# Order of weight conversion, sums of squares and normalisations in the first two blocks of a linear attention, cosine FFN and soft MoE kernel

## Chip, cores and metric

One NeuronCore of a Trainium2 chip runs the whole program. The metric is device time in microseconds, the median of several runs. Beside the runs there is one profiled execution, whose trace is read here. In it PE is TensorE's matmul stream, PEld its weight loads, DVE is VectorE, ACT is ScalarE, POOL is GpSimd and SP is SyncE, which issues most DMAs.

## What is computed

```python
kv  = einsum('bhsd,bhse->bhde', k, v)            # B=8, H=8, S=576, D=64
o   = einsum('bhsd,bhde->bhse', q, kv)
x   = o / sqrt(mean(o*o, -1) + 1e-6) * g_norm    # then as 4608 tokens x 512
h   = x @ w_in                                   # 512 x 2048, float64 weights
y   = (h * cos(h)) @ w_out                       # 2048 x 512, float64 weights
logits = y @ phi                                 # 32 slots
d   = softmax over tokens(logits); slot_in = d.T @ y
slot_out = two-layer ReLU expert per 4 slots (8 experts, 1024 hidden)
out = softmax over slots(logits) @ slot_out
```

## The kernel before

The 4608 tokens are cut into ten blocks `j` (eight of 512 tokens, two of 256), and the 2048 hidden columns into sixteen groups `f` of 128. `main(j, f)` makes the 128 x 512 product of one group with one block as 12 matmuls, since both operands are split into a high and a low part (three products for each of four slices of the depth). Its result goes through four steps: `fr_tt` (ACT, L410), `round_off` (DVE, L413), `cos_b` (ACT, L417) and `cos_c` (DVE, L456). The banks of `main` are three in rotation, so a `main` waits for the `cos_c` of three mains before.

The weights arrive as float64 bit patterns. Each group of `w_in` is converted in six steps, named by capital letters: A scales the high word (ACT, L302), R shifts it (DVE, L307), P sets the sign (DVE, L312), L sets the low bits (DVE, L317), H rounds to the high part (ACT, L323) and S subtracts for the low part (POOL, L328). `main(j, f)` needs H and S of group f. The groups of `w_out` go through the first four steps only, named `a`, `r`, `p`, `l`. Four converted groups at a time are multiplied with phi on PE: `wp_kk(c)` (L340) takes groups 4c to 4c+3. `PLAN["co"]` lists, for each group of `w_out`, the slot in which it is converted; `PLAN["wq"]=(7, 10, 13, 15)` lists the slots in which `wp_kk(0)` to `wp_kk(3)` run. `load_wout(f)` for f > 2 is issued by SP in the slot after the conversion of group f-3.

For the block after next, `att_out(j, t)` makes the attention output of 128 tokens (PE, L203), squares it (ACT, L212), sums the squares (DVE, L214 and L215) and takes the power -1/2 (POOL, L217). `att_xs` multiplies by it (DVE, L224), `att_xT` transposes (PE, L242) and rounds (ACT, L246), `att_lo` makes the low part (DVE, L255).

All this is ordered by hand: the program order of every engine is the order in which the Python code emits, and nothing reorders it. The blocks 0 and 1 are emitted by slots. Slots 0 to 3 hold block 0 alone (`PLAN["one"]`), slots 4 to 15 hold `main(0, f)` and `main(1, f-4)` (`PLAN["two"]`). A slot is a list of tokens: `m`, `f`, `r`, `b`, `c` with a digit are main and its four steps for block 0 or 1; single letters are the conversion steps (capitals for group f+2 of `w_in`, small ones for the groups of `w_out` whose `co` is f); `l`, `s`, `p`, `e` with a digit run the work that was filed beforehand under (block, f) in `loads`, `side`, `post` and `fin`. `wp_kk(0)` is filed in `side` of (0, 7), so the token `s0`, the first of slot 7, emits it ahead of `m0`. The transposes of finished groups (`gtr`, PE L497, copied by ACT at L138) and the kv sums of later batches (L184) are filed in `side` too.

```python
at2(0, PLAN["wq"][c], wp_kk, c)
for kk in range(KD):
    for o in range(4):
        f = 4 * c + o
        nc.tensor.matmul(..., rhs=half_t[f, 1][1][...], ...)
```

Of the kernel before, what the change touches and what calls it, by code (L numbers as in the profile page):

```python
# [21 lines left out]
PLAN = dict(  # L22
    ke=(0, 0),
    lp=(0, 0, 0),
    gE=(0, 0),
    co=(3, 4, 4, 5, 6, 7, 7, 8, 9, 10, 10, 11, 12, 12, 13, 13),
    wq=(7, 10, 13, 15),
    l0=(9, 9, 12, 13, 15, 15, 17, 17),
    E=((18, 19, 3, 1), (18, 19, 3, 1)),
    F=((21, 22), (21, 23)),  # L30
    L=4,
    LI=2,
    PI=2,
    start=(
# [3 lines left out]
    ),  # L38
    one='m0 e0 A R f0 P a l0 r0 p0 L r s0 b0 H p c0 S l',
    two='s0 m0 A R m1 a f0 e1 P L l0 f1 r0 r1 s1 l1 p0 r b0 H c0 e0 b1 p c1 l S p1',  # L40
    wm=(3, 5),
    pm=3,
    pa=4,
# [6 lines left out]
    A=(((0, 0, 1, 2), (1, 1, 1, 1), (2, 2, 3, 3), (0, 0, 0, 0)),  # L50
       ((9, 10, 11, 12), (0, 0, 0, 0), (11, 12, 13, 14), (0, 0, 0, 0))),
    K=((0, (0, 0, 0, 0)), (1, (1, 3, 5, 7)), (1, (13, 15, 17, 19))),
    KL=(((0, 1), (1, 2), (1, 4), (1, 6)), ((1, 11), (1, 14), (1, 16), (2, 2))),
    ao=(2, 4, 8, 11),
    xs=(1, 1, 1, 1),
    xT=(5, 8, 11, 14),
    lo=(1, 1, 0, 0),
# [8 lines left out]
TT = [n // 128 for n in SIZES]  # L66
# [6 lines left out]
def tile_linear_attention__ffn_cos__soft_moe(  # L73
# [14 lines left out]
    B, H, D = kv.shape[0], 8, 64  # L88
# [35 lines left out]
    A = A_[:, 0:512]  # L124
# [280 lines left out]
    def cos_a(j, f):  # L405
        fr_tt(j, f)
        round_off(j, f)
# [22 lines left out]
    def cos_b(j, f):  # L430
        cosine(fr_t[j, f])
# [513 lines left out]
    def at(j, f, fn, *a):  # L945
        side.setdefault((j, f), []).append((fn, a))
# [3 lines left out]
    def late(j, f, fn, *a):  # L950
        post.setdefault((j, f), []).append((fn, a))

    L = PLAN["L"]

    def U(j, f):
        if j == 0 and f >= NF:
            j, f = 1, f - L
        return j + f // NF, f % NF

    def at2(j, f, *a):  # L960
        at(*U(j, f), *a)

    def late2(j, f, *a):
        late(*U(j, f), *a)
# [11 lines left out]
    def ld_at(j, f, fn, *a):  # L976
        loads.setdefault(U(j, f), []).append((fn, a))

    for j in range(NB):
# [26 lines left out]
        if j < NB - 1:  # L1006
# [7 lines left out]
            if j < SMALL:  # L1014
                amid[U(j, la + 1)] = [(l_cross, (j,))]
                e, a, x = (U(j, k) for k in (le, la, la + 1))
# [29 lines left out]
    for b in range(1, B):  # L1046
        p, i = divmod(b, 2)
        n, sl = b - 2, PLAN["kv"]
        if b < 4:
            n, sl = PLAN["K"][b - 1]  # L1050
        for pr in range(4):
            at2(n, sl[pr], kv_pair, b, pr)

    for j in range(1, NB):
        n = min(j - 1, SMALL - 1)
        ao, dx, xt, dl = PLAN["ao"], PLAN["xs"], PLAN["xT"], PLAN["lo"]
        if n < 2:
            ao, dx, xt, dl = PLAN["A"][n]
        elif j > SMALL:
            ao, dx, xt, dl = (x[2:] for x in (ao, dx, xt, dl))  # L1060
        for t in range(TT[j]):
            i = T0[j] + t + 3
            if i < NT:
                jj = max(x for x in range(NB) if T0[x] <= i)
                ld_at(n, ao[t] + 1 + (n > 1), load_q, jj, i - T0[jj])
            at2(n, ao[t], att_out, j, t)
            late2(n, ao[t] + dx[t], att_xs, j, t)
            at2(n, xt[t], att_xT, j, t)
            at2(n, xt[t] + dl[t], att_lo, j, t)
    for b in range(2, B):  # L1070
        if b % 2 == 0:
            ld_at(*((0, 1) if b == 2 else (b - 2, 5)), load_rem, b // 2)
# [8 lines left out]
    def run(d, j, f):  # L1081
        for fn, a in d.pop((j, f), []):
            fn(*a)

    def go(j, f, ps=None):
        if (j, f) not in ran:
            run(loads, j, f)
            main(j, f, ps)
            ran.add((j, f))

    def go_next(j, f, ps=None):
        if (j, f) not in nxt:
            return None
        q, b, fns, last = nxt.pop((j, f))
        go(*q, ps)
        rest_ = []
        for fn, a in side.pop(q, []):
            if fn in fns and a[0] == b:
                fn(*a)
            else:  # L1100
                rest_.append((fn, a))
        if rest_:
            side[q] = rest_
        return b if last else None
# [8 lines left out]
    for u in range(NF):  # L1113
        n, i = 3 + u // 4, u % 4
        a, f = PLAN["nt"][i]
# [52 lines left out]
    steps = dict(A=cv_scale, R=cv_rest, P=cv_top, L=cv_low, H=cv_hi, S=cv_lo)  # L1168
# [3 lines left out]
    def ck(k, w, out):  # L1172
        need = dict(A="", R="A", P="R", L="P", H="L", S="H")[k]
        assert all((x, w, out) in done for x in need), (k, w, out)
        assert (k, w, out) not in done
        done.add((k, w, out))

    def token(t, f):
        k, *arg = t.split(".")
        if k.upper() in steps:  # L1180
            out = int(k.islower())
            ws = [int(arg[0])] if arg else [w for w in range(NF) if PLAN["co"][w] == f] if out else [f + PLAN["LI"]]
            for w in ws:
                if w < NF and (arg or out or w >= PLAN["PI"]):
                    ck(k.upper(), w, out)
# [15 lines left out]
    with tc.manual_schedule():  # L1201
        stage()
        make_identity(nc, ident)
        nc.vector.memset(mhalf, -0.5)
        nc.vector.memset(hpi, HALF_PI)
        table = sm_p.tile([128, 2], F32, tag="sb", name="table")
        nc.scalar.activation(out=table[:, 0:1], in_=mhalf[:, 0:1], func=AF.Sin)
        nc.vector.tensor_reduce(out=rep32, in_=ident.rearrange("p (j s) -> p s j", s=NS), axis=AX.X, op=ALU.add)
        nc.vector.tensor_reduce(out=quarter, in_=ident.rearrange("p (t s) -> p t s", s=NS), axis=AX.X, op=ALU.add)
        nc.vector.tensor_copy(out=rep, in_=rep32.rearrange("p (o s) -> p o s", o=1).to_broadcast([128, 4, NS]))  # L1210
        for i in range(2):
            nc.vector.memset(kz[64 - 64 * i:128 - 64 * i, i], 0.0)
        for t in kvab:
            nc.gpsimd.memset(t, 0.0)
        for t in PLAN["start"].split():
            token(t, 0)
            if t == "q.0":
                nc.sync.dma_start(out=gn, in_=gn2)
                nc.sync.dma_start(out=phi_sb, in_=phi)
        for f in range(NF):  # L1220
            if f + PLAN["LI"] + 2 < NF and f + PLAN["LI"] + 2 not in loaded:
                ld_at(0, f, load_win, f + PLAN["LI"] + 2)
            if f > 2:
                ld_at(0, min(PLAN["co"][f - 3] + 1, 12), load_wout, f)
        for f in range(NF):
            for t in (PLAN["one"] if f < L else PLAN["two"]).split():
                token(t, f)
        for j, f in [(1, f) for f in range(NF - L, NF)] + [(j, f) for j in range(2, SMALL) for f in range(NF)]:
            go(j, f)
            run(side, j, f)  # L1230
            cos_a(j, f)
            run(post, j, f)
            b = go_next(j, f)
            cos_b(j, f)
            if b is not None:
                l_exp(b)
            cos_c(j, f)
            if b is not None:
                l_sum(b)
            run(fin, j, f)  # L1240
        for j, f in [(j, f) for j in range(SMALL, NB) for f in range(0, NF, 2)]:
            if (j, f) == (NB - 1, NF - 2):
                for i in range(2):
                    ps = ps_m.tile([128, 512], F32, tag="h", name="h")[:, 0:256]
                    run(loads, j, f + i)
                    main(j, f + i, ps)
                    run(side, j, f + i)
                    if i:
                        cos_b(j, f)
                    cos_a(j, f + i)  # L1250
                cos_c(j, f)
                cos_b(j, f + 1)
                cos_c(j, f + 1)
                continue
            ps = pair_ps.pop() if pair_ps else ps_m.tile([128, 512], F32, tag="h", name="h")
            for i in range(2):
                go(j, f + i, ps[:, 256 * i:256 * i + 256])
                run(side, j, f + i)
            h_t[j, f] = ps
            cos_a(j, f)  # L1260
            for i in range(2):
                run(post, j, f + i)
            if (j, f) in nxt:
                pair_ps.append(ps_m.tile([128, 512], F32, tag="h", name="h"))
                go_next(j, f, pair_ps[0][:, 0:256])
            cos_b(j, f)
            cos_c(j, f)
            for i in range(2):
                run(fin, j, f + i)
        fill(w_p, "w15", 2)  # L1270
        fill(x_p, "x01", 4)
        for f in range(8):
            run(side, NB, f)
            run(post, NB, f)
            run(fin, NB, f)
            if f == 2:
                fill(const, "tmp0", 1)
                fill(const, "tmp1", 1)
        fill(t_p, "T1", 4)
        fill(t_p, "T0", 4)  # L1280
        tail()
        assert not any((side, post, fin, loads, amid))
# [58 lines left out]
```

## Time and profile before

| | |
|---|---|
| median of 3 runs | 666.87 us (666.53 to 667.14) |
| the profiled execution | 665.88 us |
| its span, first to last instruction | 664.1 us |
| PE busy | 642.1 us (97%) |
| DVE busy | 493.1 us (74%) |
| ACT busy | 325.1 us (49%) |
| POOL busy | 208.3 us (31%) |
| mean granted TensorE clock | 0.991 |

Times in the trace count from the span's start. A line of the timeline gives the start, the duration, the engine, the line of the code and the operation with its output and inputs; `x` counts merged instructions, and the brackets give the idle time of the engine before it and what ended it. The slots 0 to 6 lie between about 23 and 67 us.

### The profile page before, as it was taken

How to read it: one execution, taken by the hardware profiler on the slowest of the kernel's cores; microseconds unless marked ns; L12 is line 12 of the kernel's file. 1: busy time of each engine (PE TensorE's matmuls, PEld its weight loads, DVE VectorE, ACT ScalarE, POOL GpSimd, SP SyncE). 2: the span in 40 equal slices, each digit the busy share in tenths (PEclk: the TensorE clock that was granted, in tenths of full speed). 3: DMA queues.
4: the chain of work that ended last, by engine and by line, in shares of the span. 5: the costliest groups of instructions: out<-in, count | busy, mean ns of one | idle time of the engine just before them, and what ended most of it. 6: DMA issues, size and time to landing. Idle time of an engine off the chain costs nothing.

```text
span 664.1 us, 12705 instructions
## 1 busy us (share of the span) xinstructions
PE 642.1 (97%) x4689; PEld 474.8 (71%) x4689; DVE 493.1 (74%) x927; ACT 325.1 (49%) x589; POOL 208.3 (31%) x291
## 2 busy tenths in 40 slices
PE   7989999999999999999999999999999999999993
PEld 6767877877567776777677677767677778984452
DVE  3799989967577778888888888787887765546243
ACT  3577767645354454445443644544463443553032
POOL 2452111220273443542543253334426322200000
PEclk9899999999999999999999999999999999999997
DMA  8955565121395636785778376676645369999998
GB/s 318 357 202 189 177 210 172 39 69 66 73 214 144 175 81 186 197 241 134 174 204 206 98 193 185 186 213 153 157 130 123 69 178 314 320 411 407 406 408 361
DMA packets 70589, 135.13 MB, mean 203 GB/s; under 512 B 10752, under 2 KB 39040, under 8 KB 69504
## 3 DMA queue, kind: packets, MB, share of 16 engines
q1 hardware_dynamic: 63360, 119.63, 56.1%
q0 software_dynamic: 7168, 14.69, 9.7%
q8 instruction: 37, 0.61, 0.4%
q14 instruction: 24, 0.20, 0.1%
HBM read 91.29 MB, written 13.63 MB: 158 GB/s over the span
## 4 chain that ended last, share of the span: by engine, by line
PE 90%; DVE 5%; ACT 1%; issue 1%; DMA 1%; SPq 0%; DVEq 0%
PE h L392 58%; PE ab L680 5%; PE ops L203 4%; PE l L528 4%; PE kvps L184 2%; PE xTps L242 2%; PE eh L836 2%; PE eo L873 2%; PE tr L497 2%; PE l L537 2%; PE fo L902 1%; DMA kv<-in_kv 1%; DVE ss L214 1%; DVE tmp L413 1%; DVE ot L138 1%
## 5 line engine op out<-in xcount | busy, mean ns | idle before, releaser
L392 PE MATMUL h<-xt,w 128*128 128x512 f32 (+1 forms) x1920 | 423.0, 374 | 2.6 <-POOL w L328 1.0
L392 PEld LDWEIGHTS h<-xt,w 128*128 128x128 f32 x1920 | 328.8, 189 | 84.7 <-issue 11.6
L417 ACT ACTIVATE tmp<-tmp,hpi 128x512 f32<-128x512 f32 (+1 forms) x145 | 104.2, 720 | 176.6 <-DVE tmp L413 176.5
L516 POOL DMA_DIRECT2D g<-tr x224 | 123.5, 554 | 120.3 <-DVE tr L475 47.1
L456 DVE TENSOR_TENSOR gT<-tmp,h 128x512 f32<-128x512 f32 x130 | 89.0, 685 | 55.0 <-ACT tmp L417 54.5
L217 POOL TENSOR_TENSOR ri<-ss,mhalf 128x8 f32<-128x8 f32 x36 | 59.5, 1654 | 178.7 <-DVE ss L215 168.1
L413 DVE SCALAR_TENSOR_TENSOR tmp<-h,tmp 128x512 f32<-128x512 f32 (+1 forms) x145 | 97.1, 673 | 19.5 <-ACT tmp L410 18.7
L410 ACT ACTIVATE tmp<-h 128x512 int32<-128x512 f32 (+1 forms) x145 | 85.2, 587 | 44.7 <-PE h L392 42.3
L475 DVE STREAM_TRANSPOSE tr<-gT 128x512 f32<-128x512 f32 x103 | 73.2, 711 | 7.4 <-DMA g<-tr 3.3
L328 POOL TENSOR_TENSOR w<-st_m,w 128x512 fp32r<-128x512 f32 x16 | 21.3, 1333 | 63.8 <-ACT w L323 63.8
L203 PE MATMUL ops<-kvA,q 128*128 128x128 f32 (+1 forms) x320 | 38.7, 279 | 0.1
L246 ACT ACTIVATE xt<-xTps,gn 128x512 fp32r<-128x512 f32 x36 | 24.4, 683 | 27.8 <-PE xTps L242 27.8
L203 PEld LDWEIGHTS ops<-kvA,q 128*128 128x128 f32 (+1 forms) x320 | 34.5, 180 | 2.9 <-issue 1.9
L680 PE MATMUL ab<-g,d 128*32 128x512 f32 x256 | 32.2, 593 | 0.0
L528 PE MATMUL l<-gT,wp 128*32 128x512 f32 (+1 forms) x248 | 30.9, 556 | 0.0
L255 DVE SCALAR_TENSOR_TENSOR xt<-xTps,gn,xt 128x512 fp32r<-128x512 f32 x36 | 26.0, 729 | 4.8 <-ACT xt L246 4.6
L214 DVE TENSOR_REDUCE ss<-sq 128x8 f32<-128x512 f32 x31 | 21.1, 681 | 11.4 <-ACT sq L212 11.0
L212 ACT ACTIVATE sq<-ops 128x512 f32<-128x512 f32 x31 | 18.4, 594 | 19.2 <-PE ops L203 19.0
L224 DVE TENSOR_TENSOR sq<-ops,ri 128x512 f32<-128x512 f32 x31 | 20.9, 677 | 1.2 <-POOL ri L217 1.2
L680 PEld LDWEIGHTS ab<-g,d 128*32 128x32 f32 x256 | 9.6, 110 | 17.0 <-issue 15.7
L184 PEld LDWEIGHTS kvps<-kv 128*64 128x64 f32 x448 | 15.4, 137 | 8.4 <-issue 5.0
L242 PE MATMUL xTps<-ident,sq 128*128 128x128 f32 x124 | 18.9, 276 | 1.7 <-DVE sq L224 1.7
(205 smaller groups left out, 599.8 us busy)
## 6 DMA issues: line engine op xcount, KB each, us to landing
kv<-in_kv SPq DMA_DIRECT2D x28, 512.0 KB, 4.5
g<-tr SPq DMA_DIRECT2D x224, 64.0 KB, 3.7
g<-tr POOLq DMA_DIRECT2D x224, 64.0 KB, 4.0
ew<-in_ew SPq DMA_DIRECT2D x23, 512.0 KB, 8.9
q<-in_qT SPq DMA_DIRECT2D x36, 256.0 KB, 5.9
out<-ot SPq DMA_DIRECT2D x11, 768.0 KB, 6.3
rw<-in_w_in SPq DMA_DIRECT2D x16, 512.0 KB, 4.5
nat<-in_w_out SPq DMA_DIRECT2D x16, 512.0 KB, 4.3
```

The source lines that it names most:

```text
L203: nc.tensor.matmul(out=ps[p0:p0 + n, pr * 128:(pr + 1) * 128], lhsT=q_t[j, t][:, pr, p0:p0 + n], rhs=kvbd[b % 2][:, pr, :], start=True, st ...
L217: nc.gpsimd.tensor_tensor(out=ri[:, :, 0], in0=ss, in1=mhalf, op=ALU.pow)
L242: nc.tensor.transpose(ps[:, kk * 128:(kk + 1) * 128], xs[:, kk * 128:(kk + 1) * 128], ident)
L392: nc.tensor.matmul(out=ps, lhsT=w[:, a, kk, :], rhs=x[b][:, kk, :], start=(n == 0), stop=(n == 3 * KD - 1))
L410: nc.scalar.activation(out=t.bitcast(I32), in_=ps, func=AF.Copy, bias=0.25, scale=INV_2PI)
L413: nc.vector.scalar_tensor_tensor(out=t, in0=ps, scalar=INV_2PI, in1=t.bitcast(I32), op0=ALU.mult, op1=ALU.subtract)
L417: nc.scalar.activation(out=t, in_=t, func=AF.Sin, bias=hpi, scale=TWO_PI)
L456: nc.vector.tensor_tensor(out=g, in0=fr, in1=h_t.pop((j, f)), op=ALU.mult)
L475: nc.vector.transpose(out=tr_t[j, q][:, :, i, :], in_=gT_t[j, n * q + i].rearrange("p (b t) -> p b t", t=32))
L516: (nc.gpsimd if b % 2 else nc.sync).dma_start(out=dst[32 * b:32 * b + 32, :, x, a:a + n, :].rearrange("p t f i -> p t (f i)"), in_=src[32 ...
L528: nc.tensor.matmul(out=l_t[j][32 * o:32 * o + 32, :], lhsT=wp[:, f, :], rhs=gT_t.pop((j, f)), start=(c == 0), stop=(c == (2 if j == NB - 1 ...
L680: nc.tensor.matmul(out=ps[32 * c:32 * c + 32, :], lhsT=d[:, t, :], rhs=gs[c // 2][t][:, (c % 2) * 512:(c % 2) * 512 + 512], start=(t == 0) ...
```

## The change

`co` puts four of the sixteen conversions of `w_out` one slot later: group 0 from slot 3 to 4, group 2 from 4 to 5, group 3 from 5 to 6, group 6 from 7 to 8. `wq` stays. Group 2 of `w_in` is converted ahead: A in the start list, R, P and L in slot 0, H and S in the work filed for slot 0, ahead of the two `att_out` there. In slots 1 to 3 and in the two-block slots the conversion steps stand elsewhere among the steps of the mains: H and S come earlier in the two-block slots, `r` stands ahead of `r0`, and in slots 2 and 3 the DVE steps R, P, L come after `r0`. For block 1, tiles 2 and 3, `att_xs` moves from `p0` (in `post`) to `e0` (in `fin`), right behind `m0`, and the `att_lo` of block 1 are filed behind all its `att_out` and `att_xT` of a slot.

```diff
-    co=(3, 4, 4, 5, 6, 7, 7, 8, 9, 10, 10, 11, 12, 12, 13, 13),
+    co=(4, 4, 5, 6, 6, 7, 8, 8, 9, 10, 10, 11, 12, 12, 13, 13),
     wq=(7, 10, 13, 15),
-    PI=2,
+    PI=3,
-        "xs.2 L.0 H.0 S.0 xT.2 warm.3 lo.0 xs.3 lo.1 xT.3 lo.2 A.1 lo.3 R.1 P.1 L.1 H.1 S.1 "
+        "xs.2 L.0 H.0 S.0 xT.2 warm.3 lo.0 xs.3 lo.1 xT.3 lo.2 A.1 A.2 lo.3 R.1 P.1 L.1 H.1 S.1 "
-    one='m0 e0 A R f0 P a l0 r0 p0 L r s0 b0 H p c0 S l',
-    two='s0 m0 A R m1 a f0 e1 P L l0 f1 r0 r1 s1 l1 p0 r b0 H c0 e0 b1 p c1 l S p1',
+    one=(
+        'm0 e0 f0 R.2 P.2 l0 r0 L.2 s0 p0 b0 c0',
+        'm0 e0 A f0 R P l0 r0 L s0 p0 b0 H c0 S',
+        'm0 e0 A f0 l0 r0 R P L s0 p0 b0 H c0 S',
+        'm0 e0 A f0 l0 r0 R P L s0 p0 b0 H c0 S',
+    ),
+    two='s0 m0 A R m1 a f0 e1 P L l0 f1 r r0 r1 s1 H l1 p0 b0 S c0 e0 b1 p c1 l p1',
...
+    def conv(k, w):
+        ck(k, w, 0)
+        steps[k](w, 0)
+    for k in "HS":
+        at(0, 0, conv, k, 2)
...
-            late2(n, ao[t] + dx[t], att_xs, j, t)
+            (end2 if j == 1 and t > 1 else late2)(n, ao[t] + dx[t], att_xs, j, t)
             at2(n, xt[t], att_xT, j, t)
-            at2(n, xt[t] + dl[t], att_lo, j, t)
+            if j > 1:
+                at2(n, xt[t] + dl[t], att_lo, j, t)
+        if j == 1:
+            for t in range(TT[j]):
+                at2(n, xt[t] + dl[t], att_lo, j, t)
...
-            for t in (PLAN["one"] if f < L else PLAN["two"]).split():
+            for t in (PLAN["one"][f] if f < L else PLAN["two"]).split():
```

## Rows read from the trace of the kernel before

**Rows 1.** The page, 40 slices of 16.6 us: busy tenths of PE and DVE.
```profile
PE   7989999999999999999999999999999999999993
DVE  3799989967577778888888888787887765546243
```

**Rows 2.** PE's waits, whole span: releaser, us in total, times, longest.
```profile
PE xTps L242 <- DVE st_x L224: 2.3, 1, 2.3
PE xTps L242 <- DVE sq L224: 1.7, 1, 1.7
```

**Rows 3.** Timeline, PE in slots 2 to 4.
```profile
34.90 0.71 PE L392 MATMUL h<-xt,w 128*128 128x512 f32 x2
36.63 2.60 PE L392 MATMUL h<-xt,w 128*128 128x512 f32 x10 [1.02 <-POOL w L328]
39.07 0.60 PE L497 MATMUL tr<-ident,q 128*128 128x128 f32 x4
...
46.91 0.63 PE L242 MATMUL xTps<-ident,sq 128*128 128x128 f32 x4 [1.71 <-DVE sq L224]
...
47.72 5.75 PE L392 MATMUL h<-xt,w 128*128 128x512 f32 x24
```

**Rows 4.** Timeline, the other engines in slots 0 to 3.
```profile
27.18 1.06 DVE L307 TENSOR_SCALAR st_m<-st_m 128x512 int32<-128x512 int32 x1 [1.31 <-ACT st_m L302]
...
32.94 0.68 DVE L456 TENSOR_TENSOR q<-tmp,h 128x512 f32<-128x512 f32 x1
...
44.05 1.64 POOL L217 TENSOR_TENSOR ri<-ss,mhalf 128x8 f32<-128x8 f32 x1 [2.83 <-DVE ss L215]
...
46.08 0.68 DVE L224 TENSOR_TENSOR sq<-ops,ri 128x512 f32<-128x512 f32 x1
```

**Rows 5.** Timeline, PE at the end of slot 6 and in slot 7.
```profile
64.18 3.04 PE L392 MATMUL h<-xt,w 128*128 128x512 f32 x12 [0.27 <-DVE gT L456]
67.05 1.03 PE L497 MATMUL tr<-ident,gT 128*128 128x128 f32 x8
...
68.04 0.30 PE L340 MATMUL wps<-st_l,phi_sb 128*32 128x128 f32 x1
...
69.03 5.75 PE L392 MATMUL h<-xt,w 128*128 128x512 f32 x24
```

**Rows 6.** Timeline, ACT behind the last main of slot 6.
```profile
67.25 0.60 ACT L410 ACTIVATE tmp<-h 128x512 int32<-128x512 f32 x1 [1.25 <-PE h L392]
...
68.10 0.28 ACT L138 COPY we<-tr 128x128 f32<-128x128 f32 x1
...
68.82 0.73 ACT L417 ACTIVATE tmp<-tmp,hpi 128x512 f32<-128x512 f32 x1 [0.43 <-DVE tmp L413]
69.45 0.62 ACT L323 ACTIVATE w<-st_m 128x512 fp32r<-128x512 f32 x1
```

**Rows 7.** Timeline, DVE and POOL in slots 5 and 6: conversions of w_out, and S.
```profile
65.72 0.68 DVE L317 SCALAR_TENSOR_TENSOR st_l<-st,st_l 128x512 int32<-128x512 int32 x1
...
69.64 0.68 DVE L456 TENSOR_TENSOR gT<-tmp,h 128x512 f32<-128x512 f32 x1
...
70.14 1.29 POOL L328 TENSOR_TENSOR w<-st_m,w 128x512 fp32r<-128x512 f32 x1 [5.50 <-ACT w L323]
70.23 1.75 DVE L312 SCALAR_TENSOR_TENSOR st_a<-st,st_a 128x512 int32<-128x512 int32 x1
...
72.51 0.68 DVE L317 SCALAR_TENSOR_TENSOR st_a<-st,st_a 128x512 int32<-128x512 int32 x1
```

**Rows 8.** Windows of 1 and 10 us: PE, PEld, DVE, ACT, POOL busy, clock, DMA.
```profile
17.00:18.00 1.00, 0.95 (x5) 0.61 (x5) 0.97 (x3) 0.34 (x1) 1.00 (x1) 0.61 1.03 422
18.00:19.00 1.00, 1.00 (x6) 1.00 (x6) 1.00 (x2) 0.34 (x1) 1.00 (x2) 0.50 1.02 418
...
20.00:21.00 1.00, 1.00 (x8) 1.00 (x8) 1.00 (x2) 0.14 (x1) 0.07 (x1) 0.68 1.02 408
...
40.00:50.00 10.00, 8.29 (x51) 7.03 (x50) 9.93 (x18) 8.42 (x16) 4.63 (x4) 1.00 0.33 125
```

## The prediction

> **What bounds the kernel now.** I read the busy slices first. PE is full in every slice from the fourth to the last but one, while DVE comes near that only from the third to the eighth slice, about 33 to 133 us [rows 1]. So one microsecond of PE waiting is one microsecond of the kernel, and other engines matter only where PE waits for them. The list of PE's waits then says how little there is to win: the longest are 2.3 us (in the start-up) and 1.7 us for a normalised tile [rows 2], a third is 1.0 us for the low part of a weight [rows 3]; asked for 69 to 146 us alone, the list is empty. The timeline places them. In slot 2 `main(0, 2)` issues two matmuls at 34.90 and waits until 36.63 for S of weight 2; at the end of slot 3 the transpose of tile 3 waits 1.71 us until 46.91; in slot 6 `main(1, 2)` waits 0.27 us for `cos_c` to free its bank [rows 3, 5]. That is 3.0 us in all; the change aims at these. Last I read where PE meets the conversions of `w_out`: `wp_kk(0)`, which starts 0.97 us after the transposes that close slot 6 (67.05 to about 68.02; the row of its fourth operand is 68.04) [rows 5]. Its fourth operand, group 3, is ready at 66.40, the end of its step l in slot 5 [rows 7]. So it has 1.6 us to spare, and PE does not wait.
>
> **Part 1, slots 0 to 3: the waits that go.** In the trace R of weight 2 starts at 27.18, after 1.31 us in which DVE waited for A, and its own 1.06 us is long [rows 4]. A moved into the start list runs behind A of weight 1, about 23.7 to 24.4, so R and P fit into that idle time, L ends near 29.0 behind `r0`, H follows the kv copies on ACT to about 30.5, and S, with 1.29 us on POOL [rows 7], ends near 31.8. `main(0, 2)` then runs through from 34.90 and, with 2.87 us for twelve matmuls (64.18 to 67.05) [rows 5], ends at 37.8 instead of 39.07: 1.3 us won.
> Next is the chain to tile 3: two transposes and its output until 39.96 on PE, its squares on ACT to 40.7, R, P and L of weight 4 on DVE ahead of the sum of squares (it starts at 41.75 and takes 0.9), the power 1.64 us on POOL [rows 4] to 44.35, and `att_xs`, now in `e0` at the head of slot 3, 0.68 us [rows 4] to 45.2 instead of 46.76. PE, ahead by now, still waits there, some 1.5 us. A stalled `att_xs` also holds all of slot 3's DVE work behind it, since the power ends only as DVE arrives. `main(0, 4)` then starts at 46.1 instead of 47.72 [rows 3]: 1.6 us won in total. S of weight 4 (45.6) and the low parts of block 1 (48.95, for a main that wants them at 49.2) are just in time. The DMAs of `w_out` groups 3 and 4 are issued in slot 5, behind the step l that frees their buffers, as before; SP's other loads keep their slots.
> With one conversion fewer on DVE by then (three steps, of which L is 0.68 us [rows 7]) `cos_c` of slot 5 ends near 61.8, before its bank is wanted at 62.3: the 0.27 us of slot 6 go too. Gain: 1.9 us, between 0.8 (the chain to tile 3 does not shrink) and 3.0 (all three waits vanish).
>
> **Part 2, DVE in the two-block slots.** P of group 4 lasts 1.75 us beside an S on POOL that runs from 70.14 to 71.43, where other steps L and the mains' steps take 0.68 [rows 7]. With H and S earlier, S falls beside `r1` and `c0`, which show no such stretch, so DVE wins some 0.5 to 1.1 us a slot. PE waits for none of that after slot 6, so I count it as nothing; without this cover it could not bring more than the waits that PE has there, which are none.
>
> **Part 3, the later conversion of group 3.** Groups 3 and 4 now share slot 6, and `wp_kk(0)` stays first in slot 7. The step l of group 3 is emitted behind `c1` of slot 6, which hangs on the last main of that slot. Count from t, where the closing transposes start, 67.05 in the trace. ACT: `f1` at t+0.20 and two copies, the second at 68.10 [rows 6], so H can start at t+1.25; it takes 0.62 us, `b0` 0.73 [rows 6], each following at some 0.1 us less: `b0` ends at t+2.5. DVE: `c0` at t+2.52, p, p, `c1`, l, each 0.60 us after the other when back to back, so l of group 3 starts at t+4.9 and ends at t+5.6 (0.68 each [rows 7]). PE arrives at t+0.97. It waits 4.7 us. The count does not depend on part 1, since it starts from PE itself. The trace has the same place already: the l of slot 6, there of group 4, starts at 72.51 and ends at 73.19, 5.1 us behind PE's arrival [rows 7]. Bounds: 4.1 us if H falls out of ACT's way, 5.2 if S of weight 8 (t+1.8 to t+3.1) holds the first p as it did the P above. Behind the waiting matmul stand all of PE's work, `m0` of slot 7 first, and with it everything that waits for mains.
> The Trainium skill (SBUF — State Buffer, section "SBUF: two separate sides") calls the ports that VectorE and GpSimd share an exclusive lock, under which a VectorE step with two SBUF inputs is blocked by a GpSimd step until that ends. The trace agrees in the row of 1.75 us; by this rule the wait would be nearer 5.2 than 4.7.
>
> **Part 4, the clock.** After the wait of 2.3 us near the start [rows 2] the granted clock went to its lower level, 1.2 of 2.4 GHz, though PE was busy again: it is 0.61, 0.50, 0.50 and 0.68 in the four microseconds from 17 to 21, some 3.4 us at half rate [rows 8]. The wait of 1.7 us brought no fall: 1.00 from 40 to 50 [rows 8]. A wait of 4.7 us is twice the one that did, so I expect one such stretch. It costs 1.7 us if it lies on work, nothing if it lies inside the wait; being longer than the first, the wait may take a part of it. I take 1.4, with 0 and 1.7 as ends.
>
> **The sum.** Against the profiled execution, 665.88 us with a span of 664.1: -1.9 + 4.7 + 1.4 = +4.2, so about 670.1. The median of the runs is 666.87, 1.0 above it; against that, 671.1.
>
> **Rivals.**
> First, the same without the fall of the clock: 666.87 - 1.9 + 4.7 = 669.7. For it: only one earlier wait brought a fall, and the clock need not follow here. Against: this wait is twice as long. Chance 0.2.
> Second, the change does not do what it says in the early slots: the power and the sum of squares still come last, and only 0.8 us is won. Then 666.87 - 0.8 + 4.7 + 1.4 = 672.2. For it: tile 3 is normalised right after POOL's 1.64 us, and the DVE queue waits behind it. Chance 0.13.
> Third, on the other side: the conversion of group 3 is in time after all, because the wait is not PE's. This needs l of group 3 to end within 1 us of t, or PE to go on with `m0` of slot 7 while one matmul waits. The price of the wait is then nothing, no clock falls, and 666.87 - 1.9 = 665.0 is left; it turns faster once the wait is under 1.9 us. Against the first: `f1`, `b0`, `c0` and `c1` lie between and hang on PE. Against the second: at 34.90 `main(0, 2)` waited for its third matmul, and the transpose behind it, whose input had been ready since 33.6 [rows 4], came only at 39.07 [rows 3]; PE kept its order. Chance 0.07.
> The Trainium skill (TensorE: Matmul & The Clock Gate, section "Architectural detail: the array is 16× 32×32, not 1× 128×128") gives TensorE's queue a partial reorder window, which pulls weight loads ahead of running matmuls. By this rule the weights of `m0` could be taken early, not its matmuls; the trace agrees in that no matmul overtook the one that waited.
>
> **How the numbers follow.** The forecast, 671.1, has 0.6; its own ends are 669.9 and 672.7. The range for 8 in 10 reaches to the first rival's middle and the second's upper part: 668.9 to 672.8. A change under 0.2%, 1.3 us, cannot be told from none here. Faster by more needs the third rival nearly whole: 0.05. Within it lies the third rival with a short wait, or the first with all 3.0 us won and a wait at 4.1: 0.04. Slower: 0.91.
>
> **What would show it.** Right: in slot 7 a matmul of `wps` on the buffer of group 3 (`st_l`) with 4 to 5 us of idle time before it, released by DVE L317; the clock below 1 for some microseconds in or behind it; no wait at S of weight 2; `main(0, 4)` some 1.6 us earlier; no lengthened P in slots 4 to 6. Wrong: no idle PE at `wps`, a second wait of more than a microsecond in slots 4 to 15, or an idle time that starts in slots 0 to 3 because the `att_xs` in `e0` holds DVE up for POOL.

## The result and the profile after

The changed kernel takes 670.89 us (median of 6 runs, 670.04 to 671.73) against 666.53 us (6 runs of the kernel before). The ratio is 1.0068, with a 95% interval of 1.0055 to 1.0081: slower by 3.7 to 5.4 us.

| | before | after |
|---|---|---|
| median | 666.53 us | 670.89 us |
| the profiled execution, its span | 665.88, 664.1 us | 670.04, 668.2 us |
| PE busy | 642.1 us | 642.0 us |
| DVE busy | 493.1 us | 485.7 us |
| mean granted clock | 0.991 | 0.990 |

DVE has 7.4 us less to do, and the kernel is slower. First the list of PE's waits over the whole span (releaser, us in total, times, longest), of the kernel after:

```profile
PE wps L345 <- DVE st_l L322: 4.3, 1, 4.3
PE xTps L247 <- DVE st_x L229: 2.3, 1, 2.3
...
PE xTps L247 <- DVE sq L229: 1.3, 1, 1.3
```

The wait for S of weight 2 is gone, the one for tile 3 [rows 2] is 1.3 instead of 1.7 us, and at the top stands a new one: `wp_kk(0)` waits for the step l of group 3. The lines have moved by five: L340 is L345, L317 is L322, L392 is L397 and so on. The timeline of PE, kernel after, answers to [rows 3] and [rows 5]:

```profile
30.76 2.98 PE L397 MATMUL h<-xt,w 128*128 128x512 f32 x12
...
34.39 2.98 PE L397 MATMUL h<-xt,w 128*128 128x512 f32 x12
37.21 0.60 PE L502 MATMUL tr<-ident,q 128*128 128x128 f32 x4
...
44.85 0.63 PE L247 MATMUL xTps<-ident,sq 128*128 128x128 f32 x4 [1.29 <-DVE sq L229]
...
45.67 5.75 PE L397 MATMUL h<-xt,w 128*128 128x512 f32 x24
...
64.42 1.03 PE L502 MATMUL tr<-ident,gT 128*128 128x128 f32 x8
...
65.40 0.30 PE L345 MATMUL wps<-A,phi_sb 128*32 128x128 f32 x1
...
70.11 0.30 PE L345 MATMUL wps<-st_l,phi_sb 128*32 128x128 f32 x1 [4.31 <-DVE st_l L322]
...
71.55 6.89 PE L397 MATMUL h<-xt,w 128*128 128x512 f32 x24
78.28 0.60 PE L502 MATMUL tr<-ident,gT 128*128 128x128 f32 x4
```

`main(0, 2)` (34.39) runs in one piece. The operands of groups 0 to 2 are multiplied at 65.4, then PE stands until 70.11. The mains of slot 7 then take 6.73 us to the next transposes (71.55 to 78.28), where before took 5.58 (69.03 to 74.61). Windows of 1 us of the kernel after (columns as in [rows 8]) say why:

```profile
68.00:69.00 1.00, 0.00 (x0) 0.00 (x0) 1.00 (x3) 0.01 (x1) 0.00 (x0) 1.00 0.47 184
...
70.00:71.00 1.00, 0.89 (x25) 0.86 (x26) 0.66 (x2) 0.00 (x0) 0.00 (x0) 0.78 0.00 0
71.00:72.00 1.00, 1.00 (x9) 0.62 (x3) 0.00 (x0) 0.34 (x2) 0.00 (x0) 0.50 0.99 197
72.00:73.00 1.00, 1.00 (x4) 0.72 (x4) 0.44 (x2) 1.00 (x2) 0.00 (x0) 0.50 0.87 295
73.00:74.00 1.00, 1.00 (x4) 0.81 (x3) 0.97 (x2) 0.06 (x1) 0.00 (x0) 0.51 1.03 422
```

The granted clock is the third number from the end (1.00, 0.78, 0.50, 0.50, 0.51): it stays at 2.4 GHz through the wait and falls to 1.2 GHz only behind it, under work, for 3.4 us.

The two executions do not start alike: `main(0, 1)` starts at 31.23 before and at 30.76 after. So I count from that instruction to later ones that both kernels have. These are three lines that only serve as marks, of the kernel before:

```profile
31.23 3.02 PE L392 MATMUL h<-xt,w 128*128 128x512 f32 x12
...
74.61 0.60 PE L497 MATMUL tr<-ident,gT 128*128 128x128 f32 x4
...
632.99 0.70 PE sel L883 x2
```

and the last of them, from the chain that ended last, of the kernel after:

```profile
636.61 0.70 PE sel L888 x2
```

| from the start of `main(0, 1)` to | before | after | difference grows by |
|---|---|---|---|
| `main(0, 4)` | 16.49 | 14.91 | -1.58 |
| the transposes that close slot 6 | 35.82 | 33.66 | -0.58 |
| the first product with group 3 | 36.81 | 39.35 | +4.70 |
| the transposes that close slot 7 | 43.38 | 47.52 | +1.60 |
| the first select, near the end | 601.76 | 605.85 | -0.05 |

The sum is +4.09 us, and the last row says that nothing is taken or given back in the 558 us after slot 7.

### The profile page after: what moved, and what is told of

It reads as the page before. It is cut to its first block, busy times and chain, and to the rows that moved or that the text cites. A ratio compares the mean times of both kernels' runs of the same rounds, so it can differ in the third digit from the quotient of the medians.

```text
span 668.2 us, 12719 instructions
## 1 busy us (share of the span) xinstructions
PE 642.0 (96%) x4689; PEld 474.7 (71%) x4689; DVE 485.7 (73%) x927; ACT 325.7 (49%) x589; POOL 208.0 (31%) x291
## 4 chain that ended last, share of the span: by engine, by line
PE 91%; DVE 3%; DMA 2%; ACT 1%; issue 1%; POOL 0%; SPq 0%; DVEq 0%
PE h L397 60%; PE ab L685 5%; PE ops L208 5%; PE l L533 4%; PE kvps L189 2%; PE eh L841 2%; PE eo L878 2%; PE xTps L247 2%; PE tr L502 2%; PE l L542 2%; DMA kv<-in_kv 1%; DMA out<-ot 1%; PE fo L907 1%; PE wps L345 1%; DMA q<-in_qT 1%
## 5 line engine op out<-in xcount | busy, mean ns | idle before, releaser
L397 PE MATMUL h<-xt,w 128*128 128x512 f32 (+1 forms) x1920 | 423.5, 375 | 1.1 <-ACT xt L251 0.8
L397 PEld LDWEIGHTS h<-xt,w 128*128 128x128 f32 x1920 | 329.8, 189 | 82.8 <-issue 11.7
```

What stands on the lines that cost most here:

```text
L397: nc.tensor.matmul(out=ps, lhsT=w[:, a, kk, :], rhs=x[b][:, kk, :], start=(n == 0), stop=(n == 3 * KD - 1))
```

## The experiments

Each was timed together with the kernel before on the same chip; the medians of before were 666.4 to 666.8 us.

**One part alone.** The old order, with group 3 converted in slot 6 (and group 6 in slot 8, since its load follows group 3):

```diff
-    co=(3, 4, 4, 5, 6, 7, 7, 8, ...),
+    co=(3, 4, 4, 6, 6, 7, 8, 8, ...),
```

> The kernel before, with group 3 of w_out converted in slot 6 (and group 6 in slot 8, since its load follows group 3); nothing else is changed. Theory: wp_kk(0) waits for the step l of group 3, 4.5 to 5.5 us, and the granted clock falls for some 3.4 us behind it, 1.4 us more: 671.5 to 673.5 us against 666.5. Rival, that the conversion is in time or the wait has another cause (the new order of steps): 666 to 667 us and no wait at wps.

Measured: 673.47 us, ratio 1.0101 (1.0088 to 1.0115). Its trace, PE:

```profile
66.75 1.03 PE L497 MATMUL tr<-ident,gT 128*128 128x128 f32 x8
...
72.97 0.30 PE L340 MATMUL wps<-st_l,phi_sb 128*32 128x128 f32 x1 [4.84 <-DVE st_l L317]
...
74.53 6.73 PE L392 MATMUL h<-xt,w 128*128 128x512 f32 x24
```

The later conversion alone makes the wait (the product with group 3 comes 6.22 us after the closing transposes; before it was 0.99) and the slow mains, 6.57 us to the next transposes. The new order is not needed for either. The wait is 0.5 us longer than in the changed kernel. In the old order S comes later, and P of group 3 lies beside it on DVE (69.45, 1.67 us instead of 0.68), as in [rows 7]. The rows of POOL and DVE in its timeline:

```profile
69.29 1.27 POOL L328 TENSOR_TENSOR w<-st_m,w 128x512 fp32r<-128x512 f32 x1 [4.45 <-ACT w L323]
...
69.45 1.67 DVE L312 SCALAR_TENSOR_TENSOR st_l<-st,st_l 128x512 int32<-128x512 int32 x1
```

**PE keeps its order.** In the changed kernel, slot 7 alone, `main(0, 7)` ahead of `wp_kk(0)`:

```diff
+            two = PLAN["two"].replace("s0 m0", "m0 s0") if f == 7 else PLAN["two"]
```

> The changed kernel, with m0 ahead of s0 in slot 7 alone, so that main(0, 7) stands ahead of wp_kk(0) on PE. Theory: the 2.9 us of that main lie inside the time that PE waited, so 1.6 to 2.0 us of the 4.7 remain; the clock falls or not: 666.0 us without a fall, 667.6 with one. Rival, that PE takes other work past a waiting matmul anyway or that the wait moves with it: 670 to 671 us.

Measured: 666.39 us, ratio 1.0002 (0.9991 to 1.0013). The line of the wait in its trace:

```profile
70.79 0.30 PE L345 MATMUL wps<-st_l,phi_sb 128*32 128x128 f32 x1 [1.52 <-DVE st_l L322]
```

A main of 2.87 us put ahead shortens the wait by 2.8 us. So PE had stood behind a matmul that waited while the next main was ready, and took nothing past it. The clock stays at 1.00 through this wait, and the kernel is back at the time of before.

**The whole wait covered.** Both mains of slot 7 ahead of `wp_kk(0)`, which still stands ahead of the step a of group 5:

```diff
+            two = PLAN["two"].replace("s0 m0 A R m1 a f0", "m0 A R m1 f0 s0 a") if f == 7 else PLAN["two"]
```

> The changed kernel, with the tokens of slot 7 alone in the order m0 A R m1 f0 s0 a, so that both mains of the slot stand ahead of wp_kk(0) on PE, and it still stands ahead of the step a that writes group 5 over group 0. Theory: the 4.7 us of the wait lie beside 5.6 us of mains, no wait at wps and no fall of the clock are left, and the gain of slots 0 to 6 stays: 2.0 to 2.2 us less than before, 664.2 to 664.8 us against 666.5. Rival, that the wait is passed on, since group 5 and f1 of slot 7 now queue behind it: 0.5 to 2 us come back, 665 to 666.5 us.

Measured: 664.37 us (7 runs, 663.87 to 665.19), ratio 0.9967 (0.9951 to 0.9982), 2.05 us less than before (1.2 to 3.3 by the interval). In its trace the first select comes 600.10 us after the start of `main(0, 1)`, 1.66 us sooner than before. No wait at `wps` is left, and both mains of slot 7 run one behind the other:

```profile
64.75 0.60 PE L502 MATMUL tr<-ident,gT 128*128 128x128 f32 x4
65.11 5.99 PE L397 MATMUL h<-xt,w 128*128 128x512 f32 x24
70.93 0.60 PE L502 MATMUL tr<-ident,gT 128*128 128x128 f32 x4
```

So the change holds a gain of some 2 us, and one place in PE's order turned it into a loss of 4. This version beats both kernels.

**The wait moved one slot on, and lost.** `wp_kk(0)` filed in slot 8, whose place in PE's order lies behind the mains of slot 7:

```diff
-    wq=(7, 10, 13, 15),
+    wq=(8, 10, 13, 15),
```

> The changed kernel, with wp_kk(0) filed in slot 8 instead of 7. Theory: the wait at wps and the fall of the clock go, the gain of slots 0 to 6 stays, 1.9 to 2.2 us: 664.3 to 664.9 us. Rival, that the early gain is given back later by something else than this wait: 666 to 667 us.

Measured: 675.25 us, 4.4 us more than the changed kernel, and the expectation failed. Group 5 is converted in slot 7 into the buffer of group 0. Filed behind it, `wp_kk(0)` multiplies group 5 in place of group 0, and waits for the l of group 5 at the end of slot 7, for `st` instead of `st_l`:

```profile
77.52 0.43 PE L345 MATMUL wps<-st,phi_sb 128*32 128x128 f32 x2 [4.31 <-DVE st L322]
```

The same holds for the next three kernels, which are read only up to the transposes that close slot 6, ahead of that place.

**What each early part is worth.** All three on the kernel with `wq` at 8, compared with it up to the end of slot 6 (from `main(0, 1)`: 14.95 to `main(0, 4)`, 33.68 to the closing transposes).

Without the early conversion of group 2 of `w_in`:

```diff
-    PI=3,
+    PI=2,
...
-        "xs.2 L.0 H.0 S.0 xT.2 warm.3 lo.0 xs.3 lo.1 xT.3 lo.2 A.1 A.2 lo.3 R.1 P.1 L.1 H.1 S.1 "
+        "xs.2 L.0 H.0 S.0 xT.2 warm.3 lo.0 xs.3 lo.1 xT.3 lo.2 A.1 lo.3 R.1 P.1 L.1 H.1 S.1 "
...
-        'm0 e0 f0 R.2 P.2 l0 r0 L.2 s0 p0 b0 c0',
+        'm0 e0 A R f0 P l0 r0 p0 L s0 b0 H c0 S',
-    for k in "HS":
-        at(0, 0, conv, k, 2)
```

> The changed kernel with wp_kk(0) in slot 8, without the early conversion of group 2 of w_in: its steps stand in slot 0, with H and S at its end. Theory: main(0, 2) waits again for S of group 2 behind two powers on POOL, 1.0 to 1.3 us, and what follows is later by as much: 665.5 to 666.0 us. Rival, that the wait for tile 3 swallows it since both end at the same main: 664.5 us.

Measured: 15.87 us to `main(0, 4)` and 34.59 to the closing transposes. It loses 0.9 us, and `main(0, 2)` waits for S of weight 2 again:

```profile
36.44 2.57 PE L397 MATMUL h<-xt,w 128*128 128x512 f32 x10 [1.03 <-POOL w L333]
...
46.09 0.63 PE L247 MATMUL xTps<-ident,sq 128*128 128x128 f32 x4 [1.11 <-DVE sq L229]
```

A part of the loss is swallowed by the wait for tile 3, which is 0.2 us shorter.

With `att_xs` of tiles 2 and 3 behind `r0`, and the order of both slots 2 and 3 as below:

```diff
-            (end2 if j == 1 and t > 1 else late2)(n, ao[t] + dx[t], att_xs, j, t)
+            late2(n, ao[t] + dx[t], att_xs, j, t)
-        'm0 e0 A f0 l0 r0 R P L s0 p0 b0 H c0 S',
+        'm0 e0 A f0 l0 r0 p0 R P L s0 b0 H c0 S',
```

> The changed kernel with wp_kk(0) in slot 8, with att_xs of tiles 2 and 3 behind r0 instead of at the head of their slots; the filing of att_lo stays as changed. Theory: tile 3 is normalised one DVE step (0.6 us) later and its transpose with it: 665.0 to 665.3 us. Rival, that the power on POOL ends last, not the DVE queue: 664.5 us, no change.

Measured: 15.42 and 34.17 us. It loses 0.5 us, about one DVE step, and the transpose of tile 3 waits 1.88 us, where the kernel that it is compared with waits 1.29:

```profile
45.84 0.63 PE L247 MATMUL xTps<-ident,sq 128*128 128x128 f32 x4 [1.88 <-DVE sq L229]
```

So at tile 3 the place in DVE's queue counts too, and not the power on POOL alone.

With the old order in the two-block slots:

```diff
-    two='s0 m0 A R m1 a f0 e1 P L l0 f1 r r0 r1 s1 H l1 p0 b0 S c0 e0 b1 p c1 l p1',
+    two='s0 m0 A R m1 a f0 e1 P L l0 f1 r0 r1 s1 l1 p0 r b0 H c0 e0 b1 p c1 l S p1',
```

> The changed kernel with wp_kk(0) in slot 8 and with the order of before in the two-block slots (H and S late, r behind r0 and r1). Theory: DVE's P steps last over 1 us beside S again, but PE waits for none of it: the same as with the new order within 0.3 us, about 664.5 us, at most 0.3 to 0.6 us more if a main waits for its bank in slot 6 again. Rival, that the order in these slots carries part of the gain: 665.5 us or more.

Measured: 14.91 and 34.23 us. It loses nothing to `main(0, 4)` and 0.55 us between there and the end of slot 6, the upper end of what was expected. P on DVE lasts longer again beside S (62.70, 1.15 us, beside an S from 62.02 to 63.30), and the main of slot 6 waits for its bank:

```profile
62.84 3.06 PE L397 MATMUL h<-xt,w 128*128 128x512 f32 x12 [0.25 <-DVE gT L461]
```

The whole times of these three, 674.29, 674.29 and 677.31 us, say nothing on the parts.

**The order alone.** The changed kernel with the old slots of conversion:

```diff
-    co=(4, 4, 5, 6, 6, 7, 8, 8, ...),
+    co=(3, 4, 4, 5, 6, 7, 7, 8, ...),
-        'm0 e0 A f0 l0 r0 R P L s0 p0 b0 H c0 S',
+        'm0 e0 A f0 a l0 r0 R P L r s0 p0 b0 H p c0 S l',
```

> The changed kernel with the slots of conversion of before (co), group 0 again in slot 3, its four steps placed there as before had them. wp_kk(0) stays in slot 7. Theory: no wait at wps, since group 3 is converted in slot 5; the gain of slots 0 to 3 stays, less what three more DVE steps in slot 3 take from block 1's low parts, 0 to 1 us: 664.5 to 665.7 us. Rival, that the early gain needs the later conversions: 666 to 667 us.

Measured: 666.04 us, ratio 0.9989 (0.9976 to 1.0002), 0.7 us less than before, not clear of nothing. `main(0, 4)` comes as early as in the changed kernel (14.90), but then:

```profile
51.80 3.02 PE L397 MATMUL h<-xt,w 128*128 128x512 f32 x12
55.56 3.04 PE L397 MATMUL h<-xt,w 128*128 128x512 f32 x12 [0.74 <-DVE gT L461]
```

With PE ahead by 1.6 us and the conversions where they were, the second main of slot 5 waits for its bank; the closing transposes of slot 6 come at 35.04 against 33.66 in the changed kernel and 35.82 before, so that 0.8 of the 2.2 us gained stay. So the later conversions are not idle: they pay for the early gain.

**Conversions spread otherwise**, with group 3 in time, and the steps of slot 3 as in the last edit:

```diff
-    co=(4, 4, 5, 6, 6, 7, 8, 8, ...),
+    co=(3, 4, 5, 5, 6, 7, 8, 8, ...),
```

> The changed kernel with the conversions of w_out spread as 3, 4, 5, 5, 6, 7, 8, 8: group 3 is back in slot 5, group 0 in slot 3 (its four steps placed there as before had them), group 2 in slot 5. Theory: no wait at wps, and with one conversion in each of slots 3 and 4 the main of slot 5 does not wait 0.74 us for its bank, as it did with two in slot 4: 664.2 to 665.0 us against 666.5. Rival, that slot 5 with two conversions makes a new wait of a main for its bank: 665.3 us or more.

Measured: 665.81 us, ratio 0.9984 (0.9973 to 0.9995). The wait of slot 5 shrinks to 0.40 us and does not go, 1.3 us are won by the end of slot 7. The theory (no wait, 664.2 to 665.0 us) failed, and the time lies in the rival's range. But the wait is not a new one, as the rival had it: it stands at the same main as in a3_oldco, only shorter. In both traces the conversion in slot 3 stands ahead on DVE, its P lasting 1.08 us; that this holds the main up is read from the traces and was not tested by itself.

**The price of the clock.** 38 useless matmuls ahead of `wp_kk(0)`, in the changed kernel:

```diff
+                if c == 0:
+                    at2(0, PLAN["wq"][c], warm, 38)
```

> The changed kernel, with 38 more matmuls of 128x128 (about 4.2 us) in front of wp_kk(0), which fill the wait with work of no use. Theory: the wait of PE for group 3 stays as long in time, the clock stays at 1.00, and its price comes back, 1.3 to 1.7 us: 669.2 to 669.6 us against 670.9. Rival, that the clock has no price here: 670.9 us or, with the matmuls' own time, more.

Measured: 673.84 us. The matmuls took 8.65 us, not 4.2 (each takes 0.11 us, and the trace has 76 of them for the 38 in the program), so they overran the wait by some 4 us and the total decides nothing. Still, the mains of slot 7 took 5.58 us (74.81 to 80.39) with the clock at 1.00. With half as many:

```diff
+                if c == 0:
+                    at2(0, PLAN["wq"][c], warm, 19)
```

> The changed kernel, with 19 instead of 38 more matmuls (4.3 us by 8.65 us for 38) in front of wp_kk(0). Theory: they fit into the wait, the clock stays at 1.00 and 1.6 us come back: 669.3 us against 670.9. Rival, that the clock has no price: 670.9 us.

Measured: 669.83 us (5 runs, 669.70 to 670.12), 1.1 us less than the changed kernel and 0.5 us above the 669.3 that were expected. Its trace:

```profile
64.18 1.03 PE L502 MATMUL tr<-ident,gT 128*128 128x128 f32 x8
65.05 4.41 PE L810 MATMUL warm<-ident 128*128 128x128 f32 x38
70.86 5.76 PE L397 MATMUL h<-xt,w 128*128 128x512 f32 x24
76.46 0.60 PE L502 MATMUL tr<-ident,gT 128*128 128x128 f32 x4
```

The closing transposes of slots 6 and 7 lie 12.28 us apart, 13.86 in the changed kernel: 1.58 us come back where the clock stays up, as expected. By the end this execution has only 0.26 us left of them (605.59 to the first select). It loses 1.7 us against the changed kernel in one late block (a main at 442.66 us against 444.65 ahead of it, one at 481.42 against 481.71 behind it), 0.7 of them in a wait for a bank that the changed kernel does not have. Whether the early shift causes that is open.

**One more step at tile 3.** On the version of c3_late7, the sum of squares of tile 3 ahead of R, P, L in slots 2 and 3:

```diff
-        'm0 e0 A f0 l0 r0 R P L s0 p0 b0 H c0 S',
+        'm0 e0 A f0 l0 r0 s0 R P L p0 b0 H c0 S',
+            if (j, t) == (1, 3):
+                late2(n, ao[t], att_xs, j, t)
+                at2(n, max(xt), att_lo, j, t)
```

> As c3_late7, and in slots 2 and 3 the work of the side list (with the sum of squares of tile 3) stands ahead of R, P and L, att_xs of tile 3 behind them in slot 2, and all att_lo of block 1 in slot 3. Theory: the sum of squares starts 1 us earlier, the power ends near 43, and the transpose of tile 3 waits under 0.5 us instead of 1.3: 0.6 to 0.9 us less than c3_late7, 663.5 to 663.8 us. Rival, that the low parts of block 1 and S of group 5, now later on DVE and POOL, make main(1, 0) or main(0, 5) wait as long: 664.4 us or more.

Measured: 667.81 us, ratio 1.0013 (1.0002 to 1.0024), 3.4 us more than c3_late7. The theory failed, and the time lies in the rival's range, but PE does not wait where the rival said. It waits at two transposes and then, in slot 5, for the bank of `main(1, 1)`; below them stands H on ACT, which waits for the later step L:

```profile
45.23 0.63 PE L247 MATMUL xTps<-ident,A 128*128 128x128 f32 x4 [1.05 <-DVE sq L229]
46.92 0.66 PE L247 MATMUL xTps<-ident,sq 128*128 128x128 f32 x4 [1.07 <-ACT g L143]
...
58.17 3.02 PE L397 MATMUL h<-xt,w 128*128 128x512 f32 x12 [1.01 <-DVE gT L461]
...
44.70 0.63 ACT L328 ACTIVATE w<-st_m 128x512 fp32r<-128x512 f32 x1 [2.48 <-DVE st_m L322]
```

`main(0, 4)` comes 1.3 us later than in the best version (16.21 to 14.93), the closing transposes of slot 6 2.8 us (36.45 to 33.65). The copy that releases the second transpose stands behind that H on ACT. That the late H makes the delay is read from the trace, not tested.

## Why the prediction was right, step by step

The forecast was 671.1 us, +4.2 against the kernel before; +4.4 was measured between the medians and +4.09 between the two traces. That the sum of the traces is off by only 0.1 us is in part luck: the first term missed by -0.3 us and the last by +0.2, and these cancel. So is the agreement of the time itself, 671.1 to 670.89, since its base of 666.87 was a median of 3 runs, 0.3 us above that of the 6. The terms:

- **The waits that go, -1.9.** Measured -2.16. The first part was -1.6 and came out at -1.58, by the two steps named, the early weight (0.9 us by a5_w2late) and tile 3 normalised a step earlier (0.5 us by a6_oldxs); the last 0.2 us are not separated. The power and the 1.3 us that PE still waits are as worked out (1.5). The second part, the 0.27 us of slot 6, was mis-sized: it came out at 0.58, because the two mains of that slot took 6.13 us from the first to what follows (60.92 to 67.05), and take 5.55 without the wait (58.87 to 64.42). These are their first lines, before and after:

```profile
60.92 2.98 PE L392 MATMUL h<-xt,w 128*128 128x512 f32 x12
...
58.87 5.71 PE L397 MATMUL h<-xt,w 128*128 128x512 f32 x24
```

The printed idle time shows only half of what this wait cost. Where PE does not come early, one conversion fewer ahead of it is reason enough, as the prediction said: b1_co3 with the old order takes 18.84 us in slots 4 to 6, before 19.33.

- **The order in the two-block slots, nothing.** This step failed, if by half a microsecond. P no longer lasts long (in slots 4 to 6 its rows are 0.68 us, or 1.28 for two), and the text took that as worthless, since PE waits for none of it in the trace of before. But a PE that arrives 1.6 us earlier does wait: a4_oldtwo loses 0.55 us in slots 4 to 6. What was said of the conversion moved out of slot 3 needs the same correction: with the new order but the old slots of conversion, slots 4 to 6 take 20.14 us against 18.75 in the changed kernel (a3_oldco), 1.4 us longer. Both belong to the term above.
- **The wait at `wp_kk(0)`, +4.7.** Measured +4.70 (from 0.99 to 5.69 us after the closing transposes), and 4.31 in the printed wait. The chain on ACT and DVE went as counted, l of group 3 starting at t+4.95 (t+4.9 was counted), with t now 64.42. The bound of 5.2 us, in which S holds up the first p, did not come in: S had all but ended when p began, and p took its usual 0.68 us. S, that p and l, of the kernel after:

```profile
66.36 1.27 POOL L333 TENSOR_TENSOR w<-st_m,w 128x512 fp32r<-128x512 f32 x1 [5.56 <-ACT w L328]
...
67.57 0.68 DVE L317 SCALAR_TENSOR_TENSOR st_l<-st,st_l 128x512 int32<-128x512 int32 x1
...
69.37 0.68 DVE L322 SCALAR_TENSOR_TENSOR st_l<-st,st_l 128x512 int32<-128x512 int32 x1
```

In b1_co3, where S comes later, p lasted 1.67 us and the product came 5.25 us behind PE's arrival (67.72 to 72.97). b1_co3 also shows that the later conversion alone makes the wait, a7_m0first and c3_late7 that it is PE's order which makes it cost.

- **The clock, +1.4.** Measured +1.60 between the product with group 3 and the end of slot 7, and 1.58 when the wait is filled with work. The prediction let a part of the low stretch fall into the wait; here none did.

Of the rivals, the first (no fall of the clock) is not what happened, but its reason was sound, as below. The second (less gain early) is refuted by the -1.58 us. The third (in time, or PE goes past) is refuted by a7_m0first; its time of 665.0 us is near the 664.37 us that c3_late7 reaches when the wait is really covered.

## What to carry to other kernels

Where an engine works off a fixed order, ask of every step that is made later what stands first in line behind it: here PE stood 4.7 us in front of one small product while two mains were ready, and moving these ahead turned a loss of 4.4 us into a gain of some 2. Slack that nobody uses in the trace is worth something once the engine that sets the time comes earlier, so cost it against the shifted time, not against the trace. A buffer that is used again bounds how far such a product can be put off.

## What was not expected of the hardware

The wait of 2.3 us in the start-up stands in every trace of this case, and it is not always followed by the lower clock. Before, the clock fell to half from 17 to 21 us [rows 8]; after, in the same place:

```profile
17.00:18.00 1.00, 0.75 (x5) 0.57 (x6) 0.95 (x2) 0.26 (x1) 1.00 (x2) 1.00 1.06 434
18.00:19.00 1.00, 1.00 (x8) 0.82 (x8) 0.97 (x3) 0.42 (x1) 1.00 (x2) 1.00 1.00 406
```

Of the 14 profiled executions, nine show the fall and five do not. `main(0, 1)` starts at 31.04 us or later in the nine, and between 30.55 and 30.79 in four of the five; the fifth, a4_oldtwo, starts at 31.50, since its first load arrived about 1 us late. Kernels that share the code of the changed one up to slot 6 stand on both sides (a7_m0first and c3_late7 with the fall; the changed kernel, a2_warm and c4_warm19 without). So these are some 0.5 us of difference between single executions, and no edit makes them.

A wait of 4.3 us or more at `wps` was followed by the lower clock in all six executions that had one. In three of them the low stretch lasted 3.4 us, in the other three (a1_wq8, a4_oldtwo, a6_oldxs) 6.8 us, and there it began while PE still waited. Windows of 2 us of a4_oldtwo, whose wait ends at 79.95:

```profile
78.00:80.00 2.00, 0.05 (x4) 0.08 (x8) 1.80 (x3) 0.00 (x0) 0.06 (x1) 0.69 0.68 274
80.00:82.00 2.00, 2.00 (x33) 1.62 (x34) 0.00 (x0) 0.01 (x1) 0.00 (x0) 0.50 0.48 135
82.00:84.00 2.00, 2.00 (x5) 1.62 (x6) 1.10 (x2) 2.00 (x4) 0.00 (x0) 0.50 1.03 393
84.00:86.00 2.00, 2.00 (x7) 1.53 (x7) 0.71 (x2) 0.00 (x0) 0.00 (x0) 0.61 0.63 258
```

In the four kernels with `wp_kk(0)` at slot 8, PE waits 2.63 us once more, near 90 us; the lower clock followed in two (a1_wq8, a4_oldtwo) and not in the other two. A wait of 2.0 us in the start-up was followed by it in c6_xs3, and none of those of 1.0 to 1.9 us. Near the end it fell for some 3.4 us in c3_late7 and c6_xs3 (at 645 and 649 us), where PE's last wait before it was only 0.4 us. So in these traces the length of the wait alone does not tell whether the clock falls.
